# A fused RWKV-5 attention and leaky-ReLU MLP kernel on one core: fewer places for the inputs, more transpose buffers, u loaded by GpSimd, half of pair 0's first products split by chunk, and a new written order

## The chip, the cores and the metric
One core of a Trainium2 chip runs the whole kernel in one launch. The metric is the device time of one execution in microseconds (us), lower is better. The core's engines are TensorE (PE in the profile), VectorE (DVE), ScalarE (ACT), GpSimd (POOL) and SyncE (SP). Each runs its own instruction stream in order, and they wait for one another through semaphores.

## The reference, cut to what matters
There are 4 batches, 8 heads, 768 tokens and a head width of 48. Per batch and head, a 48 x 48 state is carried over the tokens, with r, k, v of the token and w, u of the head:

```
cur   = outer(u * k_t, v_t)
y_t   = r_t @ (state + cur)
state = w[:, None] * state + outer(k_t, v_t)
```

The y of all heads side by side are x (3072 tokens x 384). Then h = x @ w_in (384 x 2048), g = max(0.01 h, h), and the output is g @ w_out (2048 x 384), in float32.

## The kernel before
**Chunks and pairs.** The 3072 tokens are 24 chunks of 128 tokens, six for each batch, named n; two chunks make a pair m of 256 tokens (12 pairs). The recurrence within a chunk is turned into products: r and k are scaled by powers of w (tables qtab and ktab), multiplied to a 128 x 128 score per head, masked, and multiplied by v; the state enters at the chunk's edge.

**The written order.** Every step of the kernel has a letter and numbers, and the string ORDER lists all steps in the order in which they are recorded, for all engines together. Each engine then plays its own steps in that order. The class Sched finds for each step what it reads and overwrites, and adds the semaphore waits. Behind an @ stand the PSUM banks that the step uses; there are eight banks, and a step that opens a bank waits until its last reader is done. The steps, by letter:

- p: the start: tables, constants and first loads (list `first`, L336); q: zero the padding of a qk buffer (DVE, L374); F: filler products on a tile of ones, whose result nobody reads (PE, L381).
- k, r, v: load one chunk by a GpSimd DMA, with a cast to bf16 (L276); i, w: load a quarter of w_in and w_out (L282, L286).
- P: scale r and k of a chunk into qk (DVE, L393; for chunk 0 in two halves, P0.1 for k, L396, and P0.0 for r, L399). T and C: transpose a half on PE (L415) and copy it out (ACT, L426). X: transpose a whole chunk by a DMA from the SP queue instead (L404). Chunks 0 to 7 use T and C, chunks 8 to 23 use X.
- A: scores of a chunk (PE, L475). M: mask them (DVE, L485, L496, L499); for half of chunks 1 and 5, m copies on ACT (L506) and N masks (DVE, L512).
- D, V: the diagonal term of chunks 0 to 5, by a product for PE (DVE, L430) and a scaling of v (DVE, L554). E, f, R, L: the same term for chunks 6 to 23, by two DVE products and a DVE sum (L436, L441, L446) and a GpSimd select that writes it into the score tile (L461).
- K: keys times values (PE, L529, L533, L538). B, W: the new state (DVE, L564, L567, L572). Y: a chunk's output (PE, L603, L607). O: copy it to xT (ACT, L621).
- J and j: x times two 128-column blocks of w_in for a whole pair, six 256-column matmuls (PE, L658), and the leaky ReLU (ACT, L667). G and g: the same for one chunk and four blocks, twelve 128-column matmuls (functions `up_one` and `gate_one`, L627 and L642, not used in this ORDER).
- t, b: sums for a Strassen-like product (DVE, L710, L729). Z and z: its seven products per pair (PE, L760, eight matmuls of 192 columns each) and their additions (ACT L771, L776, DVE L781). o: store (SP L693, the last two chunks in halves, L698).

**Rings.** Buffers are reused in rings whose lengths stand in RINGS: 6 for the scaled r and k (qk), 7 for the transposed ones (tp), 14 places for loaded r and k, and 14 for v. A load into a place waits until the last reader of the chunk that held it is done.

**The start.** Chunk 0's k and r come in float32 through the ACT and SP queues (L264). w comes as a row, is spread over the partitions by a PE product (L306) and becomes the tables by a logarithm and two exponentials (L311, L363, L365), which need exponents made from an iota by GpSimd (L343, L348, L350). u comes as a row on the ACT queue (L338), is cast (L360), spread on PE (L315) and kept by ACT (L320).

Of the kernel before, what the change touches and what calls it, by code (L numbers as in the profile page):

```python
# [12 lines left out]
L = 128  # L13
# [3 lines left out]
HD = H * D  # L17
# [6 lines left out]
RINGS = (6, 7, 6, 6, 6, 3, 3, 8, 14, 14)  # L24
# [23 lines left out]
J2.0@3 r15 M8 J3.6@0 j2.0 v16 J3.4@1 E12 f12 v10 Y9@3 E10 P12 Y8@5 O9 r18 b2.0 X12 J3.0@6 j3.4 E13 O8 Z2.0@3 k17
z0.3 j3.6 f10 f13 J4.7@5 o2 z1.6 R10 k16 j3.0 J4.1@4 z0.5 R13 L10 J3.7@2 j4.1 K12@1 k15 J4.4@0 j3.7 B12 z2.0
J4.0@4 b3.0 j4.7 k19 b2.1 A10@12 j4.0 A11@56 r14 Z2.1@7 j4.4 M11 L13 Z2.2 M10 J4.6@4 k21 J4.2@0 j4.6 b2.3 k23  # L50
J4.5@5 z2.1 j4.2 b2.2 J4.3@6 j4.5 K9@4 z2.2 Z2.3@2 j4.3 B9 R12 A13@01 A12@45 M13 L12 Z3.0@6 Z2.4 z3.0 r21 W9 M12
Z2.5 v20 K10@0 Z3.1@1 B10 v18 z2.5 Y12@4 z3.1 Y10@5 W10 O12 b3.1 Y13@0 v14 Y11@7 P15 O13 K13@4 k18 O10 b4.0 Z3.2
O11 z2.3 J6.0@0 v21 E15 z3.2 z2.4 J6.6@5 f15 v17 b4.1 Z3.3@7 B13 r17 J5.1@2 b3.2 Z2.6 r16 P14 j6.0 b3.3 j5.1
J5.3@4 b4.2 Z3.4 j5.3 P18 J6.2@0 E17 E14 J5.0@2 b4.3 j6.2 J5.5@4 R15 z2.6 o5 f14 Z3.5 L15 X14 j5.5 R14 J6.3@0
j5.0 z3.4 E19 v15 P16 J6.1@3 X15 f19 L14 Z4.0@4 j6.1 Z3.6 o1 W13 X16 J6.4@2 P17 z3.6 j6.6 P19 J5.7@3 j6.4 E18 o7
K14@6 f18 Z4.1@5 j5.7 X18 z3.5 B14 j6.3 J5.4@2 z3.3 z4.0 E16 z4.1 J5.6@3 o4 W14 o0 Z4.2 j5.6 X19 A14@01 z4.2
A15@67 j5.4 M14 J5.2@3 X17 Z4.3@2 j5.2 R19 J6.7@0 M15 L19 Z4.4 k20 b5.0 K18@1 Y14@3 B18 Y15@6 R18 Z5.0@7 O15 f16
O14 b6.2 Z4.5 z5.0 j6.7 z4.4 J7.7@1 R16 Z4.6 f17 L16 z4.5 z4.3 J6.5@6 R17 o8 L18 J7.5@0 E20 o6 j6.5 o3 z4.6
A16@23 k22 j7.7 A18@56 M16 J7.2@4 L17 J7.1@1 j7.2 M18 J7.0@2 r23 j7.1 K15@3 J7.3@4 b6.0 j7.0 r20 j7.5 B15 A17@12
v19 A19@56 j7.3 b5.1 J7.4@0 M17 Z5.1@3 j7.4 Z5.2 W15 K16@4 Z6.0@0 z5.2 B16 Z6.1@1 b5.2 z6.0 z5.1 b5.3 J7.6@2 M19  # L60
Z5.3@4 j7.6 Z5.4 W16 P23 Y16@2 b6.1 Y19@5 O16 X23 Y17@6 P20 Y18@2 O17 z5.4 Z5.5 f20 O19 z5.3 O18 Z5.6 b6.3 Z6.2
# [102 lines left out]
def bass_rwkv5_eagle__then__act_leaky_relu_kernel(  # L164
# [24 lines left out]
    u_row = SB("u_row", [1, HD], FP32)  # L189
# [5 lines left out]
    k0_f = SB("k0_f", [128, HD], FP32)  # L195
    r0_f = SB("r0_f", [128, HD], FP32)
# [7 lines left out]
    u_row16 = SB("u_row16", [1, HD])  # L204
    one_row16 = SB("one_row16", [1, 128])
# [53 lines left out]
    def load_first(which):  # L259
        src = {"k": k, "r": r}[which][0].rearrange("h t d -> t h d")[0:L, :, :]  # L260
        dst = {"k": k0_f, "r": r0_f}[which]
        eng = {"k": "act", "r": "sp"}[which]
        queue = {"k": A, "r": SP}[which]
        add(eng, lambda: queue.dma_start(dst[:, :].rearrange("p (h d) -> p h d", d=D), src),  # L264
            W=[(which, 0)], dma=f"{which}0")
# [25 lines left out]
    def row(h):  # L291
        return dram(h, 0, [[HD, 1], [1, HD]])
# [571 lines left out]
```

## Time and profile before

| what | value |
|---|---|
| median of 3 runs | 165.91 us (165.53 to 166.29) |
| the profiled execution's own time | 166.21 us |
| its span in the profile | 164.1 us (2.1 us lie around it) |
| TensorE busy | 157.8 us, 96% |
| VectorE busy | 130.8 us, 80% |
| ScalarE busy | 88.6 us, 54% |
| GpSimd busy | 89.0 us, 54% |

Busy time is the time in which at least one instruction of the engine is shown running. In the timeline, a row is the start, the duration, the engine, the line, the operation, the tile written and the tile read, and how many instructions were merged; in brackets stands how long the engine had been idle before it, and what ended that. Names ending in q (SPq, POOLq) are an engine's DMA issues. PEld is the load of a matmul's stationary operand. The chain of waits is the chain of work that ended last, followed back from the end.

### The profile page before, as it was taken

The page shows a single profiled execution, that of the slowest core. Times are in us where ns is not written, and L with a number is a line of the kernel's source. Part 1 is how long each engine was busy: PE and PEld are TensorE (multiplying, and loading weights), DVE is VectorE, ACT ScalarE, POOL GpSimd, SP SyncE. Part 2 cuts the span into 40 slices and gives each one's busy share as a digit, 9 for nine tenths or more (in the row PEclk, how much of TensorE's full clock was granted, in tenths as well). Part 3 has the DMA queues.
Part 4 walks back from the last instruction along what each step waited for, and adds up shares of the span by engine and source line. Part 5 has one row for each costly group of instructions (what it writes and reads, how often), then busy time and mean ns, then how long its engine had stood idle before and what let it go on. Part 6 is the DMA issues. An engine that isn't in the chain of part 4 may idle for free.

```text
span 164.1 us, 5320 instructions
## 1 busy us (share of the span) xinstructions
PE 157.8 (96%) x2283; PEld 137.3 (84%) x2283; DVE 130.8 (80%) x261; ACT 88.6 (54%) x195; POOL 89.0 (54%) x101
## 2 busy tenths in 40 slices
PE   4899999999999899999999999999999999999993
PEld 1356778888999688899998988998989998999993
DVE  2579996999997998999997979899769960514771
ACT  3558569954862367623668256453673625738220
POOL 7999999599949969599360469000491000000000
PEclk9999999999999999999999999999999999999999
DMA  6999999999999999959999979935980000034116
GB/s 104 114 147 154 160 174 176 202 191 147 141 142 198 123 139 185 100 30 110 88 151 270 221 123 105 56 67 112 225 46 6 4 0 4 0 121 173 47 32 213
DMA packets 100091, 19.68 MB, mean 120 GB/s; under 512 B 93154, under 2 KB 100068, under 8 KB 100068
## 3 DMA queue, kind: packets, MB, share of 16 engines
q0 software_dynamic: 76512, 10.03, 93.5%
q1 hardware_dynamic: 22226, 8.92, 24.9%
q10 hardware_dynamic: 1330, 0.39, 1.0%
q8 instruction: 18, 0.29, 0.7%
q14 instruction: 5, 0.04, 0.1%
HBM read 20.45 MB, written 4.72 MB: 153 GB/s over the span
## 4 chain that ended last, share of the span: by engine, by line
PE 93%; DVE 2%; DMA 2%; issue 1%; ACT 0%; ACTq 0%; DVEq 0%
PE ps_all L658 39%; PE ps_all L760 33%; PE ps_all L603 6%; PE ps_all L475 4%; PE ps_all L381 4%; PE ps_all L415 3%; PE ps_all L533 2%; DMA u_row<-in_u_dram 2%; PE ps_all L607 1%; DVE out_sb L781 1%; DVE qk L393 1%; PE ps_all L529 0%; ACT u_row L360 0%; PE ps_all L315 0%; DVE sum_t L567 0%
## 5 line engine op out<-in xcount | busy, mean ns | idle before, releaser
L658 PE MATMUL ps_all<-xT,w_in_sb 128*128 128x256 bf16 x576 | 71.8, 273 | 0.0
L667 ACT ACTIVATE gT<-ps_all 128x512 bf16<-128x512 f32 x96 | 54.2, 604 | 31.4 <-PE ps_all L658 25.0
L658 PEld LDWEIGHTS ps_all<-xT,w_in_sb 128*128 128x128 bf16 x576 | 54.1, 98 | 6.8 <-DVE at L499 0.2
L461 POOL TENSOR_SCALAR_AFFINE_SELECT at<-s_tok 128x1024 bf16<-128x1024 f32 x18 | 21.3, 1195 | 33.8 <-DVE s_tok L446 33.7
L760 PE MATMUL ps_all<-tw,gs 128*128 128x192 bf16 x288 | 28.2, 246 | 0.0
L760 PEld LDWEIGHTS ps_all<-tw,gs 128*128 128x128 bf16 x288 | 24.0, 98 | 0.4
L499 DVE CAST_PREDICATED at<-mask,ps_all 128x1024 bf16<-128x1024 uint16 x18 | 21.5, 1216 | 2.1 <-PE ps_all L475 1.1
L781 DVE TENSOR_TENSOR out_sb<-ps_all,snap 128x192 f32<-128x192 f32 x37 | 12.5, 351 | 13.1 <-PE ps_all L760 12.9
L276 POOL DMA_DIRECT2D v_sb<-in_v_dram x24 | 22.1, 943 | 0.0
L729 DVE TENSOR_TENSOR gs<-gT 128x1024 bf16<-128x1024 bf16 x24 | 18.2, 765 | 4.6 <-ACT gT L667 4.6
L276 POOL DMA_DIRECT2D rk_sb<-in_r_dram x23 | 21.3, 939 | 0.3 <-issue 0.3
L276 POOL DMA_DIRECT2D rk_sb<-in_k_dram x23 | 21.1, 939 | 0.0
L771 ACT ACTIVATE snap<-ps_all 128x192 f32<-128x192 f32 x36 | 11.3, 333 | 18.0 <-PE ps_all L760 17.9
L760 PE MATMUL ps_all<-w_out_sb,gT 128*128 128x192 bf16 x192 | 19.3, 246 | 0.0
L621 ACT ACTIVATE xT<-ps_all 128x384 bf16<-128x384 f32 x24 | 11.1, 496 | 10.4 <-PE ps_all L603 8.6
L760 PEld LDWEIGHTS ps_all<-w_out_sb,gT 128*128 128x128 bf16 x192 | 15.9, 98 | 0.7
L393 DVE TENSOR_TENSOR qk<-rk_sb,tab 128x768 bf16<-128x768 bf16 x23 | 15.3, 685 | 0.0
L426 ACT ACTIVATE tp<-ps_all 128x512 bf16<-128x512 f32 x16 | 9.0, 604 | 5.0 <-PE ps_all L415 5.0
L603 PE MATMUL ps_all<-at,v_sb 128*32 128x128 bf16 x384 | 10.5, 220 | 0.1
L603 PEld LDWEIGHTS ps_all<-at,v_sb 128*32 128x32 bf16 x384 | 8.2, 96 | 2.4 <-issue 1.3
L760 PE MATMUL ps_all<-w_out_sb,gs 128*128 128x192 bf16 x96 | 9.9, 246 | 0.0
L446 DVE TENSOR_REDUCE s_tok<-ku 128x8 f32<-128x384 bf16 x18 | 9.7, 544 | 0.1
(69 smaller groups left out, 184.3 us busy)
## 6 DMA issues: line engine op xcount, KB each, us to landing
out_dram<-out_sb SPq DMA_DIRECT2D x22, 192.0 KB, 2.2
v_sb<-in_v_dram POOLq DMA_DIRECT2D x24, 96.0 KB, 5.0
rk_sb<-in_r_dram POOLq DMA_DIRECT2D x23, 96.0 KB, 5.2
rk_sb<-in_k_dram POOLq DMA_DIRECT2D x23, 96.0 KB, 5.3
w_in_sb<-in_moe_w_in_dram POOLq DMA_DIRECT2D x4, 384.0 KB, 5.9
w_out_sb<-in_moe_w_out_dram POOLq DMA_DIRECT2D x4, 384.0 KB, 10.3
tp<-qk SPq DMA_TRANSPOSE x16, 4.3
k_f<-in_k_dram ACTq DMA_DIRECT2D x1, 192.0 KB, 2.9
```

The costliest lines, as they stand in the source:

```text
L276: add("pool", lambda: G.dma_start(dst, src), W=[key], dma=f"{which}{n}")
L393: add("dve", lambda: V.tensor_tensor(qk[iq][:, :, 0:D], both, by, ALU.mult), R=[("r", n % NRK), ("k", n % NRK), "qtab", "ktab", ("qk0", iq ...
L461: add("pool", lambda: G.affine_select(out=at[ia][:, :, :, :].rearrange("p two m i -> p (two m) i"), in_=s_tok[i2][:, :].unsqueeze(2).to_br ...
L499: add("dve", lambda: V.copy_predicated(dst, mask[:, :].bitcast(mybir.dt.uint16).unsqueeze(1).to_broadcast([128, H, 128]), raw), R=keys + [ ...
L603: last = PE.matmul(ps_y[32 * q:32 * q + 32, 128 * s:128 * s + 128], a, m, start=first_mm and (s == 0 or whole), stop=last_mm and whole)
L621: add("act", lambda: A.activation(xT[m % NX][:, :, 128 * half:128 * half + 128], ps[i][:, 0:HD].rearrange("p (s t) -> p s t", t=128), AF.C ...
L658: last = PE.matmul(ps[i][:, 256 * f:256 * f + 256], w_in_sb[:, s, 128 * fb:128 * fb + 128], xT[ix][:, s, :], start=s == 0, stop=s == NSL - 1)
L667: add("act", lambda: A.activation(gT[ig][:, 2 * j:2 * j + 2, :].rearrange("p f t -> p (f t)"), ps[i][:, :], AF.Prelu, alpha=0.01), R=[key] ...
L729: add(eng, lambda: on.tensor_tensor(x[i][:, :, :], a, b, op), R=keys, W=[("gs", m % 2, i)])
L760: done = PE.matmul(ps[i][:, 0:NH], lhs[:, s, :], rhs[:, s, :], start=bool(opens) and s == 0, stop=s == HF - 1, skip_group_check=not (opens ...
L771: add("act", lambda: A.activation(snap[i2][j][:, :], ps[i][:, 0:NH], AF.Copy), R=[key], W=[("snap", i2, j)])
L781: add("dve", lambda: V.tensor_tensor(out_sb[io][:, cols], ps[i][:, 0:NH], snap[i2][j][:, :], ALU.add), R=[key, ("snap", i2, j), *after], W ...
```

## The change
- RINGS go from (6, 7, 6, 6, 6, 3, 3, 8, 14, 14) to (8, 10, 6, 6, 6, 3, 3, 8, 10, 12): qk 8 for 6, tp 10 for 7, places of r and k 10 for 14, of v 12 for 14.
- u is no longer a row that ACT casts, PE spreads and ACT copies. One GpSimd DMA reads it 128 times into u_tab, with the cast.
- Chunk 0's float32 k and r land in output tiles 5 and 4 instead of tiles of their own.
- J0.0 to J0.3 and their j become G0.0, G0.1, G1.0, G1.1 and their g: blocks 0 to 7 for chunk 0 and chunk 1 separately.
- ORDER is new throughout: the order of the steps on every engine, and the banks. The fillers are 17 with 4864 columns for 28 with 9728.

```diff
-RINGS = (6, 7, 6, 6, 6, 3, 3, 8, 14, 14)
+RINGS = (8, 10, 6, 6, 6, 3, 3, 8, 10, 12)
+FIRST = {0}
 ORDER = """
-p3 p0 p9 p12 q0 p2 p18 p1 r3 p11 p13 p14 p10 p4 p8 p5 p21@0 k3 p6 p20 k1 p7 p25@1 F1.256.0@2 p22 r1 F1.128.4@3
-F1.128.5@4 F1.512.8@2 p24 F1.256.12@0 k2 F1.512.15@7 P0.1 F1.256.4@0 F1.512.16@2 p17 r2 p27 p15 p23 p19 q5
-F1.512.4@0 q4 q3 F1.512.6@7 P0.0 i1 p28 F1.256.9@0 p16 T0.1@2 v0 T0.0@0 F1.512.12@3 C0.1 p32 p31 F1.512.7@4 q1
-F1.512.0@3 k5 C0.0 P1 p29 A0@23 D0 p30 r5 F1.512.5@0 q2 M0.0 F1.256.16@7 F1.512.19@6 T1.0@0 v1 P2 F1.128.2@4
...
+p3 p0 p19 p10 r1 p2 p8 p16 p4 r2 p11 p5 p21@0 p6 k1 p7 F1.512.12@1 k2 F1.128.19@2 p22 F1.512.18@1 F1.128.3@7 i1
+F1.128.21@6 F1.128.17@5 F1.256.4@7 F1.512.17@0 p9 v0 F1.512.11@1 p13 q0 p24 p18 q1 F1.128.7@0 F1.512.1@7 q5 p14
+p31 p17 p23 k3 p15 F1.128.6@6 P0.1 F1.128.0@7 F1.256.5@5 p27 F1.512.6@4 p28 P0.0 r3 F1.256.9@3 q2 T0.0@2 P1
+T0.1@1 C0.0 F1.128.8@0 P2 v1 T1.0@7 T1.1@0 C0.1 k5 C1.0 D0 A0@12 p32 T2.0@6 C1.1 q3 M0.0 T2.1@7 r5 p29 p30 q4
+M0.1 C2.1 v2 K0@5 C2.0 A1@01 D1 V0 m1.1 i0 A2@67 B0 Y0@4 v3 P3 O0 M1.0 K1@5 k4 N1.1 T3.1@1 G0.1@0 V1 C3.1 r4
+T3.0@2 P5 Y1@1 C3.0 i3 D2 B1 A3@23 O1 k7 M2 g0.1 K2@4 T5.0@5 v4 G1.1@1 C5.0 V2 r7 D3 Y2@0 M3.1 i2 T5.1@7 M3.0
+G0.0@6 C5.1 r6 B2 K3@5 O2 G1.0@7 g1.1 V3 p1 q7 Y3@4 P4 k6 B3 T4.0@3 O3 T4.1@2 v6 D5 A5@01 C4.1 q6 J1.0@5 M5.0
...
+j6.7 A15@45 j6.5 A14@67 J6.4@2 M14 j5.6 K14@0 J6.3@3 j6.4 P22 z4.0 J6.1@6 j6.3 M15 X22 J6.2@7 j6.1 Z4.1@2
+P17 j6.2 X18 R18 Z4.2 R19 L18 K15@3 B14 Z4.3@4 z4.2 X20 z4.1 W14 r23 Z4.4 B15 Z4.5 z4.3 L19 X17 R16 Y15@0 z4.4
+v20 Y14@7 b6.0 O15 X16 A18@34 O14 E17 A19@56 v16 M18 Z4.6 K18@0 v17 o3 J7.3@7 z4.6 b6.1 o4 o7 J7.2@1 L16 b5.0 o2
...
+z8.6 Z9.5 o17 z9.4 Z11.0@0 b11.2 Z10.1@5 z9.5 z11.0 b11.1 Z11.1@7 b10.3 Z10.2 Z11.2@3 z10.2 z11.1 z10.1 Z10.3@2
+z11.2 b11.3 Z10.4 Z10.5 z10.4 Z10.6 z10.5 z10.3 Z9.6 z10.6 Z11.3 z9.6 o19 Z11.4 z11.3 o18 z11.7 o16 Z11.5 z11.4
+o23.1 o21 Z11.6@2 o20 z11.5 o23.0 o22.1 z11.6 o22.0
 """
...
+    def early(which, n):
+        return out_sb[4 + 2 * n + (which == "k")][:, :]
...
-    def load_first(which):
+    def load_early(which, n, eng):
...
+    def first_u():
+        add("pool", lambda: G.dma_start(u_tab[:, :], dram(u, 0, [[0, 128], [1, HD]])), W=["u_tab"], dma="u")
...
-    def spread_u():
-        i, key = opened("u")
-        add("pe", lambda: PE.matmul(ps[i][:, 0:HD], one_row16[:, :], u_row16[:, :], start=True, stop=True),
-            R=["one_row16", "u_row16"], W=[key, "bc16"])
-
-    def keep_u():
-        i, key = banks["u"]
-        add("act", lambda: A.activation(u_tab[:, :], ps[i][:, 0:HD], AF.Copy), R=[key], W=["u_tab"])
```

In the new ORDER, GpSimd's iota (p9) stands behind five loads (r1, r2, k1, k2, i1); in the old one it stood ahead of all loads.

More of the change, by code (lines that the diff above doesn't have):

```diff
@@ L52 @@
[L52 to L61, printed above, removed]
@@ L306, in spread_w @@
         add("pe", lambda: PE.matmul(ps[i][:, 0:HD], one_row[:, :], w_row[:, :], start=True, stop=True),
-            R=["one_row", "w_row"], W=[key, "bc"])
+            R=["one_row", "w_row"], W=[key])
     def log_w():
@@ L359, in bass_rwkv5_eagle__then__act_leaky_relu_kernel @@
         lambda: add("dve", lambda: V.memset(wu[:, :, :], 0.0), W=["wu"]),
[L360 removed]
+        None,
         spread_w,
```

103 lines of the change are left out of this document (50 added, 53 removed).

## The prediction

> **What bounds the kernel now.** I read the page's busy shares and chain of waits, then busy time by stretches, then the timeline where the stretches show something.
>
> ```profile
> PE 157.8 (96%) x2283; PEld 137.3 (84%) x2283; DVE 130.8 (80%) x261; ACT 88.6 (54%) x195; POOL 89.0 (54%) x101
> ...
> PE 93%; DVE 2%; DMA 2%; issue 1%; ACT 0%; ACTq 0%; DVEq 0%
> ```
>
> PE is busy for 96% of the span and makes 93% of the chain that ended last: a change pays where it takes work off PE or lets it wait less. The stretches (us; busy us of PE, PEld, DVE, ACT, POOL, with instructions) show where:
>
> ```profile
> 8.51:24.40 15.89, 15.80 (x271) 11.00 (x269) 14.64 (x34) 10.35 (x21) 15.89 (x19) 1.00 2.08 159
> 24.40:108.80 84.40, 83.76 (x1315) 74.76 (x1313) 78.45 (x145) 48.73 (x106) 59.03 (x64) 1.00 1.57 141
> 108.80:161.59 52.79, 52.76 (x688) 49.17 (x688) 33.58 (x68) 25.95 (x62) 6.50 (x6) 1.00 0.32 72
> ```
>
> The first stretch begins with the first real product. After it PE is idle for 0.64 us in 84.40 and 0.03 in 52.79. In the middle stretch DVE works 78.45 us and is idle for only 5.95: **a second limit stands close behind PE**. After 108.80 DVE has 19 us to spare. The first stretch looks full of PE work too, but its rows with L381 are filler, which nobody reads:
>
> ```profile
> by line: PE ps_all L381 42.3%; PE ps_all L415 27.6%; PE ps_all L475 13.8%; PE ps_all L533 4.5%; PE ps_all L603 4.2%; PE ps_all L529 3.8%; PE ps_all L607 3.2%; issue 0.7%
> ...
> 9.36 1.28 PE ps_all L381 x3
> ...
> 11.10 0.65 PE ps_all L381 x3
> 11.74 0.22 PE ps_all L415 x4
> ...
> 15.37 0.36 PE ps_all L603 x16
> ```
>
> This is the chain from 8.51 to 17.1, after which no filler comes; its first row gives L381 42.3% of 8.59 us, so 3.63 us. The others are pieces of it: start, us, line, instructions. The fillers cover waits for the pipeline of a chunk (transpose, copy, scores, mask, output). Dropping them gains nothing unless real work takes their place.
>
> **The change, step by step.** *Half of the first products per chunk.* J0.0 to J0.3 need xT of chunks 0 and 1; G0.0 and G0.1 need chunk 0 alone. A J is six matmuls of 256 columns, a G twelve of 128:
>
> ```profile
> 23.74 0.66 PE ps_all L658 x6
> ...
> 44.50 0.66 PE ps_all L760 x8
> ...
> 107.29 1.51 PE ps_all L603 x100
> ```
>
> A J takes 0.66, four 128-column matmuls 0.22 (row 11.74), so a G 3 x 0.22 = 0.66: no PE time is won or lost, and ACT still does four leaky ReLUs of 128x512. What it brings is a date.
>
> *The start.* Both tables need exponents from the iota, which now stands behind five loads on GpSimd.
>
> ```profile
> 0.90 0.23 POOL L343 IOTA ramp<- 128x128 f32 x1 [0.39 <-POOLq L849]
> 1.41 1.04 POOL L276 DMA_DIRECT2D rk_sb<-in_r_dram  x1 [0.27 <-issue]
> 2.44 1.76 POOL L276 DMA_DIRECT2D rk_sb<-in_k_dram  x2
> 5.12 0.61 ACT L365 ACTIVATE tab<-lnw,kexp 128x384 bf16<-128x384 f32 x1
> ...
> 6.44 0.51 DVE L352 TENSOR_SCALAR ident<-ramp 128x128 bf16<-128x128 f32 x1
> ```
> ```profile
> 2.34 1.64 PE L306 MATMUL ps_all<-w_row,one_row 1*128 1x384 f32 x2 [2.34 <-DMA w_row<-in_w_dram]
> 4.70 0.49 PE L315 MATMUL ps_all<-u_row,one_row 1*128 1x384 bf16 x1 [0.71 <-ACT u_row L360]
> ```
>
> Loads follow each other by 1.03 or 0.88 (half of 1.76). Five from 0.95 on end at 0.95 + 1.03 + 4 x 0.88 = 5.5, and the iota at 5.75, for 1.13. ktab (0.61) then ends at 6.5 for 5.73. DVE has small memsets, the mask and ident (0.51 in its row) ahead of chunk 0's two scalings, which then run at about 7.3 and 7.8 for 0.5 each, and the transposes T0 start at 8.35, for 8.51. The new fillers ahead of them, 4736 columns, fit: at the 0.83 ns per column of row 9.36 (1536 columns in 1.28) they take 3.9 us from the end of the w product (2.34 + 1.64 = 3.98). Bounds of T0's start: 7.9 (the fillers' end) to 9.4 (ident's 0.51 for each of the small ones). I take 8.35, to which the row of the old scalings is nearest.
>
> *The first chunks, walked along.* Start to start DVE needs, from these rows, 0.46 for V (14.72 to 15.18) and P, 0.47 for B, 0.34 for D and as much for N, 0.61 for a half M (17.77 to 18.38) and at most 1.21 for a whole one; ACT needs 0.51 per copy (2.06 for four) and 0.37 per wl; a load of v lands 5.0 us after its issue in the median, 10.9 at most:
>
> ```profile
> 14.72 0.55 DVE L554 TENSOR_TENSOR vs<-v_sb,ps_all 128x384 bf16<-128x384 bf16 x1
> 15.18 0.55 DVE L564 TENSOR_TENSOR st<-ps_all,wl 128x384 bf16<-128x384 f32 x1
> 15.65 0.55 DVE L393 TENSOR_TENSOR qk<-rk_sb,tab 128x768 bf16<-128x768 bf16 x1
> 16.11 0.42 DVE L430 TENSOR_TENSOR prod<-tp 128x512 bf16<-128x512 bf16 x1
> 16.45 0.42 DVE L512 TENSOR_TENSOR at<-at,mask 128x512 bf16<-128x512 bf16 x1
> ...
> 17.77 0.68 DVE L485 TENSOR_TENSOR at<-ps_all,mask 128x512 bf16<-128x512 f32 x1
> 18.38 0.55 DVE L564 TENSOR_TENSOR st<-ps_all,wl 128x384 bf16<-128x384 f32 x1
> 18.84 1.21 DVE L496 TENSOR_TENSOR at<-ps_all,mask 128x1024 bf16<-128x1024 f32 x1
> ```
> ```profile
> 10.08 0.74 ACT L327 ACTIVATE wl<-lncol 48x192 bf16<-48x192 f32 x2
> ...
> 12.93 2.06 ACT L426 ACTIVATE tp<-ps_all 128x512 bf16<-128x512 f32 x4 [0.33 <-PE ps_all L415]
> ```
> ```profile
> DMA to landing us min/median/max: 3.1/5.0/10.9
> ```
>
> T0 (0.44 for both halves, by row 11.74) ends at 8.8, its copies at 9.8, A0 at 10.15. DVE masks A0 until 11.6, then D1 and V0 until 12.4. ACT copies chunk 1, makes wl, copies chunk 2 until 12.5; A2 stands ahead of Y0 on PE, so Y0 runs from 12.85 to 13.45 (15.37 to 16.00 before), its copy ends at 14.0, and G0.1 starts at 14.1. From there DVE sets the pace: V1 ends at 14.75 and Y1 at 15.8; P5 (whose r lands near 15.2: issued near 10.1), D2 and B1 end at 16.5, M2 and V2 at 18.1, Y2 at 18.9; D3, M3, B2 and V3 at 20.5, Y3 at 21.45. G1.1, G0.0 and G1.0 lie in the gaps; A5 ends at 21.8. The old kernel has done the same products (chunks 0 to 3, A5, four units of w_in) when its fourth J ends, at 23.74 + 0.66 = 24.40. **PE is 2.6 us ahead.** Bounds: 3.63 if all filler turns into progress; nothing if the start slips by one and each of some eight hand-overs costs 0.2 more than I gave.
>
> *The middle.* Up to the last Y of chunks 16 to 19 (row 107.29 ends at 108.80) the old order has 42 Z, the new one 39, at 0.66 each (row 44.50); otherwise PE has the same. So PE needs 83.76 - 1.98 = 81.8 us from 21.8 on: 103.6 if it never waits. DVE has, at 21.8, not yet done what it had at 24.40: N5.1, E6, P6, part of D5 and P7, some 1.3 us; up to those Y the new order has two b less and an E and a P more, 0.5 less (between 0 and 1; the b are the longer ones). So it must work 78.45 + 1.3 - 0.5 = 79.3 us, and only 81.8 - 79.3 = **2.5 us of idle** are left to it, for 5.95 before. DVE's idle time was waiting for PE; both in-order streams rarely wait for nothing, so I take the middle, 4.2 us: 21.8 + 79.3 + 4.2 = 105.3. PE's one visible stop of before is an instance of the coupling:
>
> ```profile
> 53.36 1.93 DVE L393 TENSOR_TENSOR qk<-rk_sb,tab 128x768 bf16<-128x768 bf16 x1
> 53.74 1.12 POOL L461 TENSOR_SCALAR_AFFINE_SELECT at<-s_tok 128x1024 bf16<-128x1024 f32 x1
> ...
> 55.61 0.40 PE L475 MATMUL ps_all<-tp 48*128 48x128 bf16 x8 [0.62 <-DVE out_sb L781]
> ```
>
> DVE's P took 1.93 us instead of 0.55 beside GpSimd's select, so a bank came free late and PE stood for 0.62. The Trainium skill (SBUF — State Buffer, section "Who interferes with whom") says that a DVE instruction with two SBUF inputs and a GpSimd one that reads SBUF take one lock, held for the whole instruction; these rows agree. By that rule alone the two orders could be told apart by what stands right behind each sum R on DVE: a two-SBUF-input step 10 times in 18 before, 8 times now, which would save DVE about 1 us; the sum does without it.
>
> *The rest.* After those Y, 52.79 + 1.98 = 54.8 us follow to the last product, then 164.10 - 161.59 = 2.5 to the end. On the SP queue five whole stores now stand within the last four Z, ahead of the last half, for three before: two more of 192 KB, between 0 and 1 us later; I take 0.2, since they are issued earlier.
>
> *At nothing.* u by GpSimd: a load's 0.9 us on GpSimd, issued at about 20.5 and wanted by E7 near 28; it takes a product of 0.49 off PE (row 4.70), ahead of fillers, and would cost only if it landed over 7 us later. Chunk 0 in output tiles: the outputs that overwrite them come 40 us later. Two more zero memsets on DVE, 0.3, lie in its idle time. More qk and tp buffers free SP of waits that PE didn't feel. Fewer places: each load after the start goes out at least 6 us of PE work ahead of its use, for a median landing of 5.0; the longest, 10.9, would be felt by a few.
>
> **Sum.** Y17 at 105.3 + 54.8 + 2.5 + 0.2 = span 162.8, that is 1.3 less than 164.1. The profiled execution took 166.21, the median is 165.91: I predict **164.6** for the median.
>
> **The rivals.**
> (a) PE never waits: span 103.6 + 57.5 = 161.1, time 162.9. For it: the old order kept PE waiting for 0.64 only. Against: DVE would have to be 97% busy for 82 us. Chance 0.15.
> (b) DVE waits as much as before, 5.95: 107.05 + 57.5 = 164.55, time 166.35: the gain of the start given back. The point is 5.5 us of idle. Chance 0.17.
> (c) Slower: the DMA transpose of chunk 18. Between X18 and A18 PE has four Z, K15, Y15 and Y14, 4 x 0.66 + 0.2 + 2 x 0.45 (four Y take 1.51 in row 107.29) = 3.7 us; the shortest such distance in the old order is 5.7.
>
> ```profile
> L404 SPq DMA_TRANSPOSE tp<-qk x16: 1236/1304/1995, 47.2 to 115.0; - x16
> ...
> DMA to landing us min/median/max: 3.2/4.3/6.1
> ```
>
> Issue takes 1.3 us, landing 4.3 in the median and 6.1 at most, and four others go out around it. From a landing of 3.7 + 1.3 = 5.0 the gain is gone; at 6.1 PE stands for 2.4 us: span 165.2, time 167.0, and more if chunk 18's masks then hold up the neighbours'. Chance 0.20.
> (d) PE stays slow longer. Row 9.36 has 0.83 ns per column, row 11.10 0.51 (1280 columns), though PEclk shows 1.00 throughout; PE had been busy without a gap from 4.7 to 10.64. The new start has gaps of some 0.4 to 0.9 us from 9.4 on. If it runs at half speed until 15, 4.0 us of products become 8.0, and 2.3 are lost: time 166.9; up to 168.6 if until 18. The Trainium skill (TensorE: Matmul & The Clock Gate, Part 1) says that the clock is halved until a window of 3.4 us was busy, and again after an idle one; by that rule the new fillers, without the old gap of 0.71 ahead of row 4.70, have PE at full rate by 9.4, which is nearly what the walk takes. Chance 0.08.
> (e) The change doesn't do what it says: the G wait for w_in. The quarter wanted at 14 is the fifth load, issued by 5.5: no weight.
>
> **How the numbers follow.** The forecast has 0.40 and by itself reaches from 163.4 to 165.4. A measurement tells about 0.5%, 0.83 us, from no change. Faster by more: (a) and three quarters of the forecast, and little of the rest, 0.47. Within: the rest of the forecast and most of (b), 0.23. Slower: (c), (d), some of (b), 0.30. The range reaches from (a), less 0.7 for a start that is earlier by its bound and stores that cost nothing, 162.2, to the upper end of (d), 168.6.
>
> **What would show it.** Right: L381 filler after the first transpose near zero, G0.1 near 14, Y3's end near 21.5, DVE idle of 3 to 5 us between there and Y17. Wrong: a PE wait for T0 after 9.4; A18 late behind a DMA; PE idle over 3 us after 25.

## The result: 174.1 us, slower by 4.9%

The changed kernel takes **174.10 us** (median of 4 runs, 173.35 to 175.30), the kernel before beside it 165.72 (165.51 to 166.29): ratio 1.0494, 95% interval 1.0449 to 1.0539. Predicted were 164.6 us, between 162.2 and 168.6. The profiled execution took 173.35 with a span of 171.6. Ratios are formed from the runs within 1.5% of the fastest of the same kernel, but medians and ranges are of all runs, since the changed order spreads by 3% by itself (171.2 to 176.6 us in e13 below).

Busy shares and the chain of waits of the changed kernel, from its page:

```profile
PE 156.0 (91%) x2295; PEld 137.8 (80%) x2295; DVE 127.8 (74%) x262; ACT 88.8 (52%) x193; POOL 90.2 (53%) x102
...
PE 46%; DVE 23%; DMA 16%; POOL 7%; issue 5%; ACT 1%; DVEq 0%; POOLq 0%
PE ps_all L754 19%; PE ps_all L652 19%; DMA tp<-qk 9%; DMA rk_sb<-in_k_dram 6%; DVE gs L723 4%; DVE qk L387 4%; PE ps_all L597 3%; POOL rk_sb L278 3%; PE ps_all L469 2%; DVE at L493 2%; POOL at L455 2%; DVE tw L704 2%; POOL v_sb L278 2%; DVE ku L430 1%; DVE sum_t L561 1%
```

PE no longer carries the chain: 46% for 93% before. DMAs have 16% of it: the DMA transposes (tp<-qk) have 9%, loads of k 6%. Line numbers are six lower than before (L652 is J, L754 Z, L597 Y, L469 A, L387 the scaling P, L398 the DMA transpose), and in most of the experiments eight lower.

Stretches as in the prediction (us; busy us of PE, PEld, DVE, ACT, POOL, then granted clock): from the end of A5 to the last Y of chunks 16 to 19, and from there to the last product.

```profile
22.60:111.01 88.41, 82.99 (x1284) 74.19 (x1284) 77.96 (x146) 48.27 (x106) 64.34 (x69) 0.98 1.78 151
111.01:167.62 56.61, 55.02 (x712) 51.10 (x710) 32.86 (x69) 27.39 (x63) 4.43 (x4) 1.00 0.16 41
```

Laid beside the prediction's own sum, stage by stage:

| stage | predicted | profile after | difference |
|---|---|---|---|
| to the end of A5 | 21.8 | 22.60 | +0.8 |
| A5 to the last Y of chunks 16 to 19 | 83.5 | 88.41 | +4.9 |
| to the last product | 54.8 | 56.61 | +1.8 |
| to the end of the span | 2.7 | 171.6 - 167.62 = 4.0 | +1.3 |
| span | 162.8 | 171.6 | +8.8 |

In the middle PE is idle for 88.41 - 82.99 = 5.42 us (0.64 before), in the third stage for 1.59 (0.03). DVE was to be the second limit there; it worked 77.96 us (79.3 forecast) and was idle for 10.45. The largest piece, in order of time on PE (start, us, line, operation, count, idle time before):

```profile
54.06 0.33 PE L527 MATMUL ps_all<-v_sb,qk 128*128 128x96 bf16 x4
58.11 0.62 PE L469 MATMUL ps_all<-tp 48*128 48x128 bf16 x16 [3.71 <-DMA tp<-qk]
58.66 1.45 PE L652 MATMUL ps_all<-xT,w_in_sb 128*128 128x256 bf16 x6
59.91 1.48 PE L754 MATMUL ps_all<-w_out_sb,gT 128*128 128x192 bf16 x8
61.19 1.28 PE L754 MATMUL ps_all<-tw,gT 128*128 128x192 bf16 x8
62.40 0.28 PE L469 MATMUL ps_all<-tp 48*128 48x128 bf16 x4
```
```profile
58.66:62.40 3.74, 3.74 (x25) 3.02 (x24) 2.82 (x3) 0.93 (x2) 3.74 (x5) 0.54 1.70 146
62.40:66.00 3.60, 3.60 (x94) 3.15 (x94) 3.09 (x4) 1.21 (x3) 1.95 (x3) 1.00 2.02 148
```

The scores of chunk 9 wait 3.71 us for their DMA transpose. Behind the stop one J and two Z take 62.40 - 58.66 = 3.74 us where 3 x 0.66 would do, and the second view says why: the granted clock was 0.54 there and 1.00 afterwards. The stop costs 3.7 + 1.8 us. The six DMA transposes of chunks 8 to 13, before and after (issue ns min/median/max, first and last start; us to landing):

```profile
L404 SPq DMA_TRANSPOSE tp<-qk x6: 1236/1295/1937, 47.2 to 59.2; - x6
...
DMA to landing us min/median/max: 4.1/4.9/6.1
```
```profile
L398 SPq DMA_TRANSPOSE tp<-qk x6: 1391/2551/4057, 44.3 to 57.7; - x6
...
DMA to landing us min/median/max: 6.8/8.6/9.5
```

They go out 3 us earlier, are issued half as fast and take almost twice as long. When the first goes out, 10 loads of r, k and v are issued but not landed; 5 were before (counted from each load's issue and landing in the trace).

The third stage and the end belong together: the stores. SP issues eight whole rows in a block, while the load of k23 is under way.

```profile
99.76 7.17 SPq L687 DMA_DIRECT2D out_dram<-out_sb  x8
```
```profile
L278 POOL DMA_DIRECT2D rk_sb<-in_k_dram x1: 919/919/919, 101.9 to 101.9; - x1
...
  DVE ku L430: 3.1, 1
...
DMA to landing us min/median/max: 11.0/11.0/11.0
```
```profile
119.13 0.83 PE L754 MATMUL ps_all<-w_out_sb,gT 128*128 128x192 bf16 x8 [1.15 <-DVE sum_t L561]
...
121.06 0.61 PE L652 MATMUL ps_all<-xT,w_in_sb 128*128 128x256 bf16 x4 [0.44 <-DVE sum_t L561]
```

k23 lands 11.0 us after its issue, DVE stands 3.1 us for it, the state sums come late, and PE stops for 1.15 + 0.44 = the 1.59 us of the third stage.

### The profile page after: what moved, and what is told of

Read it like the earlier page. It is cut to its first block, busy times and chain, and to the rows that moved or that the text cites. A ratio compares the mean times of both kernels' runs of the same rounds, so it can differ in the third digit from the quotient of the medians.

```text
span 171.6 us, 5349 instructions
## 1 busy us (share of the span) xinstructions
PE 156.0 (91%) x2295; PEld 137.8 (80%) x2295; DVE 127.8 (74%) x262; ACT 88.8 (52%) x193; POOL 90.2 (53%) x102
## 4 chain that ended last, share of the span: by engine, by line
PE 46%; DVE 23%; DMA 16%; POOL 7%; issue 5%; ACT 1%; DVEq 0%; POOLq 0%
PE ps_all L754 19%; PE ps_all L652 19%; DMA tp<-qk 9%; DMA rk_sb<-in_k_dram 6%; DVE gs L723 4%; DVE qk L387 4%; PE ps_all L597 3%; POOL rk_sb L278 3%; PE ps_all L469 2%; DVE at L493 2%; POOL at L455 2%; DVE tw L704 2%; POOL v_sb L278 2%; DVE ku L430 1%; DVE sum_t L561 1%
## 5 line engine op out<-in xcount | busy, mean ns | idle before, releaser
L661 ACT ACTIVATE gT<-ps_all 128x512 bf16<-128x512 f32 x92 | 51.9, 603 | 32.8 <-PE ps_all L652 31.0
L652 PE MATMUL ps_all<-xT,w_in_sb 128*128 128x256 bf16 x552 | 66.6, 274 | 0.4 <-DVE sum_t L561 0.4
L652 PEld LDWEIGHTS ps_all<-xT,w_in_sb 128*128 128x128 bf16 x552 | 52.5, 98 | 7.8 <-DVE sum_t L561 0.7
L455 POOL TENSOR_SCALAR_AFFINE_SELECT at<-s_tok 128x1024 bf16<-128x1024 f32 x18 | 22.1, 1244 | 26.2 <-DVE s_tok L440 26.1
L754 PE MATMUL ps_all<-tw,gs 128*128 128x192 bf16 x288 | 28.2, 246 | 0.0
L754 PEld LDWEIGHTS ps_all<-tw,gs 128*128 128x128 bf16 x288 | 24.1, 98 | 0.2
L754 PE MATMUL ps_all<-w_out_sb,gT 128*128 128x192 bf16 x192 | 20.3, 251 | 1.2 <-DVE sum_t L561 1.2
L775 DVE TENSOR_TENSOR out_sb<-ps_all,snap 128x192 f32<-128x192 f32 x37 | 12.2, 348 | 9.5 <-PE ps_all L754 7.6
L615 ACT ACTIVATE xT<-ps_all 128x384 bf16<-128x384 f32 x24 | 10.8, 494 | 15.4 <-PE ps_all L597 13.5
L754 PEld LDWEIGHTS ps_all<-w_out_sb,gT 128*128 128x128 bf16 x192 | 16.5, 100 | 2.0 <-DVE sum_t L561 1.4
L469 PE MATMUL ps_all<-tp 48*128 48x128 bf16 x192 | 8.3, 218 | 6.3 <-DMA tp<-qk 5.0
L387 DVE TENSOR_TENSOR qk<-rk_sb,tab 128x768 bf16<-128x768 bf16 x23 | 12.4, 543 | 1.1 <-DMA rk_sb<-in_r_dram 1.1
L469 PEld LDWEIGHTS ps_all<-tp 48*128 48x128 bf16 x192 | 5.5, 94 | 8.7 <-issue 4.1
L597 PE MATMUL ps_all<-at,v_sb 128*32 128x128 bf16 x384 | 10.6, 220 | 0.5 <-DMA v_sb<-in_v_dram 0.4
L754 PE MATMUL ps_all<-tw,gT 128*128 128x192 bf16 x96 | 10.2, 253 | 0.0
```

The source lines that it names most:

```text
L387: add("dve", lambda: V.tensor_tensor(qk[iq][:, :, 0:D], both, by, ALU.mult), R=[("r", n % NRK), ("k", n % NRK), "qtab", "ktab", ("qk0", iq ...
L455: add("pool", lambda: G.affine_select(out=at[ia][:, :, :, :].rearrange("p two m i -> p (two m) i"), in_=s_tok[i2][:, :].unsqueeze(2).to_br ...
L469: last = PE.matmul(ps[i][:, 128 * p:128 * p + 128], tp[it][at_rows, NP + p, :], tp[it][at_rows, p, :], start=True, stop=True)
L597: last = PE.matmul(ps_y[32 * q:32 * q + 32, 128 * s:128 * s + 128], a, m, start=first_mm and (s == 0 or whole), stop=last_mm and whole)
L652: last = PE.matmul(ps[i][:, 256 * f:256 * f + 256], w_in_sb[:, s, 128 * fb:128 * fb + 128], xT[ix][:, s, :], start=s == 0, stop=s == NSL - 1)
L661: add("act", lambda: A.activation(gT[ig][:, 2 * j:2 * j + 2, :].rearrange("p f t -> p (f t)"), ps[i][:, :], AF.Prelu, alpha=0.01), R=[key] ...
```

## The experiments

Theory: the new order puts DMA transposes into a backlog of loads, and loads behind a block of stores. Rivals: the smaller number of places; DVE as the bound; the new start. "Outstanding" are loads of r, k and v that are issued and have not landed when the first transpose goes out. A ratio is to the kernel before, run beside the experiment. Each profile shows one execution.

**e1, e14: more places.**
```diff
-RINGS = (8, 10, 6, 6, 6, 3, 3, 8, 10, 12)
+RINGS = (8, 10, 6, 6, 6, 3, 3, 8, 13, 14)
```


> The changed kernel, its order untouched, with 13 places for r and k instead of 10 and 14 for v instead of 12. Theory (order of the transfers: DMA transposes stand on the SP queue and in time where the loads are still backed up, and stores ahead of late loads): GpSimd no longer waits for places (4.3 us for r22 and 2.6 us for v22 in the changed kernel), but loads only go out earlier; PE's stop before A9 near 54 us stays at 3 to 4.5 us, the stops near 118 to 121 stay within 1 us of 1.6, and the time stays at 172.5 to 175.5. Rival (fewer places): the stops after 80 us go and the stop before A9 shrinks under 1.5 us, time 167 to 170.

Measured: 171.13 us (169.95 to 171.68), ratio 1.0302 (1.0237 to 1.0367). A9 did not wait at all (the longest stop of PE between 40 and 66 us was 0.30, before A11), against the theory; the late stops stayed (1.04 and 0.44), against the rival. But in that execution the fourth chunk's output was copied at 23.7 us instead of 21.9, and the first transpose went out at 46.2 with 7 loads outstanding. That left it open, and e13, e14 and e15 were put side by side on one chip.

> The changed kernel itself, once more, beside e14 and e15 on one chip. Theory (a lead of PE at the start brings the first DMA transposes forward into a backlog of loads that the DMA engines set): 172.5 to 175.5; the number of loads outstanding when X8 is issued, and the landings of X8 to X13, follow the lead of this execution as in the others (10 or 11 outstanding: over 6.8 us; 7: 4.4 to 7.7).

> e1 once more. Theory (places bind only after 65 us, and e1's missing stop before A9 came from a shorter lead in that execution): 171 to 174, at most 2 us under e13. Rival (places are worth the 3 us that e1 showed): 169.5 to 171.7, 2.5 to 4 us under e13 in all runs.

Measured: e13 174.27 us (171.16 to 176.60), e14 173.24 (171.72 to 174.98). The same six transposes, e13 and then e14:

```profile
L398 SPq DMA_TRANSPOSE tp<-qk x6: 1342/2501/4642, 46.2 to 61.0; - x6
...
DMA to landing us min/median/max: 6.7/9.0/10.1
```
```profile
L396 SPq DMA_TRANSPOSE tp<-qk x6: 1346/2518/3724, 46.1 to 59.1; - x6
...
DMA to landing us min/median/max: 6.6/8.4/9.1
```

10 and 9 loads outstanding, stops before A9 of 4.23 and 3.31 us: with 13 and 14 places the stop is there all the same. The places cannot have set it: up to r12, at 45.7 to 45.8 us, GpSimd issues every load at the same time within 0.12 us in e1, e13 and e14. Nor did the lead of PE, which both theories name, tell these three apart: the first transpose went out at 46.1 or 46.2 us in each. What differed is when the loads landed: w0, issued at 23.6 us in each, landed at 31.4 in e1, at 34.4 in e13 and at 33.6 in e14. The times leave open what places are worth behind A9. e14 is 1.0 us under e13, and all ten runs of e1 and e14 have a median of 171.9 us, those of the changed kernel and e13 174.3.

**e2: fewer places in the old order** (11 and 12 for 14 and 14 in the kernel before).

> The kernel before, its order untouched, with 11 places for r and k and 12 for v instead of 14 each (with 10, r22 would stand ahead of the last use of r12 in this order). Theory (order of the transfers): within 1 us of the kernel before, 165 to 167. Rival (fewer places): a good part of the 8 us of loss shows, 168 us or more, with waits of GpSimd on places and PE stops behind late loads.

Measured: 166.65 us, before 166.13; ratio 1.0028 (0.9996 to 1.006). As the theory said: in the old order the places alone cost nothing that can be told.

**e15, e9: three loads later.**
```diff
 order of GpSimd's loads
-r13 v13 k10 k8 r8 r9 k11 k9 r10 r11 r16 v8 v9 v12 k12 r12 v10 k16 k19 r19 v19 v11
+r13 k10 k8 r8 r9 k11 k9 r10 r11 v8 v9 k12 r12 v10 k16 k19 r19 v19 v11 v12 r16 v13
```


> The changed kernel with three loads that are wanted late (v13, r16, v12) moved behind v11 on GpSimd, out of the backlog ahead of the first DMA transposes; nothing else. So far the transposes of chunks 8 to 13 took 3.5 to 6.1 us to land where 5 or 6 loads were outstanding at the issue of the first, 4.4 to 7.7 with 7, 6.8 to 8.0 with 8, 6.8 to 9.5 with 10 and 7.3 to 11.0 with 11. Theory (transposes among outstanding loads land late): 7 or 8 outstanding here, landings of 4.4 to 8 us, PE's stop before A9 under 2 us, and 1.5 to 4 us less than the changed kernel: 170 to 172.5. Rival (it is the order of X13, X8, X9 on the SP queue, or a place, that holds A9): 173 to 175 with a stop over 3 us.

Measured: 174.09 us (171.41 to 183.65). Its profiled execution, the one of 183.65, had a granted clock of 0.85 nearly throughout, so its times can't be compared, but its transposes of chunks 8, 9, 10 and 13 landed in 3.1 to 3.5 us with 4 loads outstanding. Hence once more:

> e9 once more, whose profiled execution had a granted clock of 0.85 and can't be read for times. Theory (backlog of loads ahead of the first transposes): 4 to 8 loads outstanding at X8, landings of X8 to X13 under 6 us but for X11, X12, no stop before A9 over 1 us, 1.5 to 4 us under e13. Rival: within 1 us of e13.

Measured: 171.57 us (170.79 to 172.80), 2.7 under e13 by the medians; one run of e13 lies in the same range, and the ratios, 1.0281 (1.0227 to 1.0336) and 1.032 (1.022 to 1.042) in e13, don't tell the two apart. The transposes in e15:

```profile
L396 SPq DMA_TRANSPOSE tp<-qk x6: 1234/1340/2616, 45.7 to 55.8; - x6
...
DMA to landing us min/median/max: 3.8/5.7/7.7
```

The first issue is as in e13 within 0.5 us, on the same queue, in the same order; 7 loads are outstanding instead of 10. The median landing falls from 9.0 to 5.7, the issue time from 2.5 to 1.3 us, and the longest stop at a score product from 4.23 to 0.66. It was not a quicker execution: r13, issued at 28.3 us, landed at 41.6 as in e14, but chunk 9's transpose landed at 53.5 us for 59.3 there. **The backlog of loads makes the transposes late.** In all four executions with the three loads moved (e9, e15, e10, e16) A9 never waited; of the five with these loads, the order of the transposes and PE's work as in the changed kernel, four waited for 3.31 to 5.20 us (the changed kernel, e8, e13, e14) and one did not (e1). Across all executions of the changed order and its variants, landings (min to max of the six) rise with the loads outstanding:

| kernel | loads outstanding | to landing, us | longest PE stop, 40 to 66 us |
|---|---|---|---|
| before | 5 | 4.1 to 6.1 | 0.62 |
| e9 (clock 0.85) | 4 | 3.1 to 5.9 | under 0.1 |
| e10 | 6 | 3.4 to 7.3 | 0.49 |
| e1, e15, e16 | 7 | 3.7 to 7.7 | 0.56 |
| e4 | 8 | 6.8 to 8.0 | 3.0, filled |
| e14 | 9 | 6.6 to 9.1 | 3.31 |
| after, e13 | 10 | 6.7 to 10.1 | 4.23 |
| e7, e8 | 11 | 7.3 to 11.0 | 5.20 |

The gain in time is less sure than the mechanism: all ten runs of e9 and e15 have a median of 171.9 us, no less than those with more places.

**e4: filler in the stop.** 14 products of 512 columns, read by nobody, ahead of A9.
```diff
-j3.7 B8 r19 K9@6 z1.5 j3.6 A9@23
+j3.7 B8 r19 K9@6 z1.5 j3.6 F14.512.0@2 A9@23
```


> The changed kernel with 14 products of 512 columns that nobody reads put on PE just ahead of the scores of chunk 9 (3.0 us at full rate, inside the stop of 3.7 us). Theory (the wait is for the transpose's landing, and PE runs slow after the stop): the scores of chunk 9 start at the same time, but the J and Z after them take 0.66 per six and eight matmuls at once instead of 1.38 and 1.18, so the time falls by 1 to 2 us, to 172 to 173. Rival (the products after the stop are slow for another reason, a bank or operand): no change, 173.5 to 174.5; and if PE's own work were what A9 waited for, the time would rise by 3.

Measured: 172.92 us (171.41 to 173.55), 1.2 under the changed kernel's median. PE there:

```profile
55.71 2.97 PE L373 MATMUL ps_all<-ones 128*128 128x512 bf16 x13
58.61 0.62 PE L467 MATMUL ps_all<-tp 48*128 48x128 bf16 x16
59.16 0.83 PE L650 MATMUL ps_all<-xT,w_in_sb 128*128 128x256 bf16 x6
59.83 0.82 PE L752 MATMUL ps_all<-w_out_sb,gT 128*128 128x192 bf16 x8
60.49 0.82 PE L752 MATMUL ps_all<-tw,gT 128*128 128x192 bf16 x8
61.24 0.40 PE L467 MATMUL ps_all<-tp 48*128 48x128 bf16 x8
```

A9 starts at 58.61 (58.11 without filler), and the J and two Z behind it go by every 0.66 us at a granted clock of 1.00: behind filler instead of a stop, the stop's second cost, the slow clock, falls away. That useless work shortens the kernel is not shown. In this execution chunk 9's transpose had landed at 56.8 us, so that A9 would have waited for 1.1 us and the filler held it back for 1.8; and the times lie within the spread of the changed kernel (171.16 to 176.60 with e13).

**e7: X13 moved.**
```diff
 SP's queue
-X8 X13 X9 X10 X11 X12
+X8 X9 X10 X11 X12 X13
 DVE: P13 likewise behind P12
```


> The changed kernel with the scaling and the DMA transpose of chunk 13 moved behind those of chunk 12; nothing else. Theory (A9 waits for a transpose that stands behind two others among the loads): X9 goes out in X13's old place, 2.7 us sooner, and lands near 54; PE's stop before A9 falls from 3.7 to under 1.2 us and the slow products behind it go; time 169 to 171.5. Rival (fewer places, or the backlog of loads alone): X9 lands as late as before, near 58; 173 to 175.

Measured: 174.88 us (170.53 to 175.26). X9 went out 0.6 us sooner than in the changed kernel, landed at 55.2 instead of 58.0, and A9 no longer waited. But the time stayed, for another stop of 2.95 us took its place, before A10 (59.0 to 62.0 us). DVE, then GpSimd:

```profile
56.40 3.21 DVE L385 TENSOR_TENSOR qk<-rk_sb,tab 128x768 bf16<-128x768 bf16 x2
59.54 1.24 DVE L564 TENSOR_TENSOR st<-sum_t,wl 128x384 bf16<-128x384 bf16 x1
60.70 2.34 DVE L491 CAST_PREDICATED at<-mask,ps_all 128x1024 bf16<-128x1024 uint16 x2
```
```profile
58.06 2.50 POOL L453 TENSOR_SCALAR_AFFINE_SELECT at<-s_tok 128x1024 bf16<-128x1024 f32 x2
```

The scalings of chunks 12 and 13 take 3.21 us (twice 0.55 alone), 2.35 of it the second, which with the state product of 1.24 (0.35 alone) runs beside two selects of GpSimd from 58.06 to 60.56; the mask on which a bank hung came late. It is the stretching that the prediction showed for one P of 1.93 us. The theory was right on A9 and wrong on the time: mending one transpose only moved the stop. Whether the 11 loads outstanding or the new place of the scaling brought it there is not shown.

**e8: stores earlier.**
```diff
 SP's queue
-X8 X13 X9 X10 X11 X12 X21 X15 X14 X19 o1 o0 X22 X18 X20 X17 X16 o3 o4 o7 o2 o5 o9 o6 o8 X23 ... o17 o19 o18 o16 o21 ...
+X8 X13 X9 X10 X11 X12 o3 o2 o0 o1 o4 o5 X21 X15 X14 o6 X19 o7 X22 X18 X20 X17 X16 o9 o8 X23 ... o16 o17 o18 o19 o21 ...
```


> The changed kernel with the whole-row stores on the SP queue moved to where their rows are ready: o0 to o3 and o4, o5 into the gap of the SP queue between 60 and 80 us, o6, o7 among the transposes, o16 and o18 ahead of o19; nothing else. Theory (stores that go out in a block delay what is behind them): k23 lands within 7 us instead of 11, the stops near 118 and 121 (1.15 and 0.44 us) go, and the end comes 2.6 us after the last product instead of 4.0; 2 to 3 us less, 171 to 172.5. Rival (those loads are late because GpSimd waits for places): stops and time stay but for the end, 172.5 to 174.5.

Measured: 171.53 us (169.28 to 172.68), ratio 1.0185 (1.0095 to 1.0274). The load of k23:

```profile
L276 POOL DMA_DIRECT2D rk_sb<-in_k_dram x1: 919/919/919, 104.8 to 104.8; - x1
...
DMA to landing us min/median/max: 5.3/5.3/5.3
```

5.3 us for 11.0. In all eight executions that keep the block of stores k23 takes 10.3 to 11.3 us, in the three without it (e8, e10, e16) 5.0 to 5.9. There is no stop after 109 us; the span ends 170.81 - 167.90 = 2.9 us after the last product for 4.0. As the theory said, 2.6 us less by the medians, although its profiled execution had the longest stop before A9 of all (5.20 us).

**e10, e16: loads and stores; and places besides.**

> The changed kernel with both: the three loads of e9 later and the stores of e8 earlier. Theory (two separate losses, one of backlog ahead of the transposes, one of stores ahead of late loads and at the end): the gains add up, 1.5 to 4 from the one and 2.6 to 3.6 from the other: 167 to 170, with no stop over 0.6 us after O15. Rival (the same loss, which moves from place to place): no better than the better of the two, 170 to 172.5.

> e10 (three loads later, stores earlier) with 13 places for r and k and 14 for v. Theory (with ten places GpSimd waits 4.3 us for the place of r22 and all loads behind it, and P14 and P15 with their transposes are late: e10 still stops 1.17 us for X14 and 0.60 for v11): those stops fall under 0.5 us each and the time is 1 to 2 us under e10: 167.4 to 168.4. Rival (the place is not what those loads wait for): 169 to 170, the stops stay.

Measured: e10 169.39 us (168.55 to 171.73), ratio 1.0128 (1.0038 to 1.0218); e16 169.68 (168.40 to 170.41), ratio 1.0157 (1.01 to 1.0214). The two gains add up (4.7 us under the changed kernel), and places add nothing on top: the rival of e16 holds. The edits are those of e9 and e8, in e16 with the places of e1. What is left of the loss in e16 are waits of one to two us with different causes (us in total, times, longest):

```profile
PE ps_all L521 <- DMA v_sb<-in_v_dram: 1.8, 1, 1.8
PE ps_all L467 <- DMA tp<-qk: 1.0, 2, 0.8
PE ps_all L752 <- DVE gs L721: 0.9, 1, 0.9
PE ps_all L467 <- DVE s_tok L438: 0.9, 1, 0.9
```

Two of them end with DVE, the prediction's second limit.

**e3, e5, e6, e11: the new start with the old rest.**
```diff
 e3
-RINGS = (8, 10, 6, 6, 6, 3, 3, 8, 10, 12)
+RINGS = (6, 7, 6, 6, 6, 3, 3, 8, 14, 14)
 new order as far as g1.0
-the rest of the new order
+j1.0 j1.2 j1.3, then all other steps as the kernel before has them, without J0.0 to J0.3
```

> The new start and first half of pair 0's products (u by GpSimd, chunk 0 in output tiles, G instead of J, everything up to the mask of chunk 5), then all remaining steps in the order of the kernel before, with the places and buffers of the kernel before (14, 14, 6, 7). Theory (order of the transfers from 40 us on): the start's lead of about 1.8 us survives, no PE stop over 1.5 us after 25 us; time 163.5 to 166. Rival (DVE is the bound and takes the lead back): 165.5 to 167 with PE stops spread over the middle and DVE idle under 4 us. Rival (the new start itself costs): 168 or more, with the stops after 25 us.

Measured: 169.73 us, ratio 1.024 (1.0167 to 1.0313). The theory's range is missed at the joint, where the two orders meet: E6 stands early in the old order, while its load k6 stands late in the new one.

```profile
29.20 0.36 DVE L428 TENSOR_TENSOR ku<-rk_sb,u_tab 128x384 bf16<-128x384 bf16 x1 [4.61 <-DMA rk_sb<-in_k_dram]
```

DVE stood 4.61 us, PE 3.14, and PE's granted clock was 0.50 from 30.42 to 36.00. After that there is no stop over 0.30 us.

```diff
 e5: the new order as far as f6 (for g1.0), then as e3
 e6: besides, GpSimd's first loads
-r1 r2 k1 k2 i1 (iota) v0 k3
+r1 r2 k1 k2 v0 i1 (iota) k3
```


> As e3, but the new order is kept until the second product of chunk 6's sum (f6, about 37 us), so that E6 and P7 come only after their loads; from there on all remaining steps in the order of the kernel before, places and buffers of before. Theory (the loss sits in the transfers of the new order from 43 us on, and e3's stop was its joint, where E6 asked for k6 eight loads too early): no PE stop over 1 us after 25 us, chunks 16 to 19 done 0 to 2 us ahead of the kernel before; time 164 to 166. Rival (the new start costs later whatever follows, since DVE or the loads take the lead back): 166.5 or more, with stops in the middle.

> e5 with one load moved: v of chunk 0 goes out ahead of the first quarter of w_in instead of behind it. Theory (the start is set by landings: the first K waits for v0, 0.3 to 1.3 us in the runs so far, and the gap makes the products after it slow): v0 lands near 9 us, the gap before the first K shrinks to what DVE needs, output of chunk 0 is copied before 13.9 us every time; 0.3 to 1.2 us less than e5. Rival (that gap is hidden by what DVE does next): same time as e5 within 0.3 us.

Measured: e5 166.13 us, ratio 0.9968 (0.9932 to 1.0005); e6 166.07, ratio 0.9962 (0.9932 to 0.9993). With the rest in the old order the 8 us are gone, though e5 comes out 0.1 above the theory's range. In e6 v0 lands at 9.5 us for 12.2 and the first K no longer waits for it, but the time is that of e5: the rival. The edit has a price of its own: the iota now stands behind one load more, and T0 starts at 9.08 us for 8.21.

```diff
 e11: as e6, and
-GpSimd: k13 v7 w2 w1 w3 r13 v13 k10 k8 k9
+GpSimd: k8 v7 w2 w1 w3 r13 k9, with k10, k13, v13 as in the kernel before
-PE: J0.5 A7 A6 Y5
+PE: A7 A6 Y5 J0.5
-DVE: E8 t0 t2 t1 E9 t3
+DVE: t0 t2 t1 E9 t3 E8
```


> e6 (new order up to f6, old order for the rest, v0 first) with the joint mended: k8, k9, k10, k13, v13 loaded in the old sequence, J0.5 behind Y5, E8 behind the sums of w_out. Theory (PE work lost at the joint, 0.58 + 0.69 + 0.20 us of stops, comes back in full because nothing else is late): 0.8 to 1.5 us less than e6, 164.6 to 165.4. Rival (DVE or the transposes take it back between 45 and 60 us): 165.7 to 166.3.

Measured: 165.67 us (165.23 to 166.64), kernel before beside it 166.17; **ratio 0.9959 (0.992 to 0.9997)**. It lies between the two ranges. It is 0.4 us under e6 on another chip, but by the ratio to the kernel before beside it (0.9962 in e6) the mended joint gains nothing that can be told, though the profiled span fell by 0.9. It clearly beats the changed kernel, and the one before by 0.4%, with an interval that just excludes no change. Most of the start's lead is gone by the end; where it goes stays open.

**e12: the iota first.**
```diff
 e11, GpSimd
-r1 r2 k1 k2 v0 i1 (iota) k3 r3 v1 k5 r5 v2
+(iota) r1 k1 v0 k2 r2 v1 i1 k3 r3 v2 r5 k5
```

> e11 with the start in another order: the iota first on GpSimd, then r1, k1, v0, k2, r2, v1, and w_in only then; the small steps of DVE in the order in which they are wanted, and the fillers ahead of the first transpose cut from 4736 to 3328 columns. Theory (with the iota behind the loads the exponent table, and with it the first transpose, is late by 1.5 us): T0 starts near 6.6 instead of 8.2 to 9.1 us, and what the loads of chunks 1 to 5 allow of it remains: 0.3 to 1.5 us less than e11. Rival (the loads' landings set the first 24 us, whatever the start): the same time as e11 within 0.3 us.

Measured: 166.39 us, ratio 0.9992 (0.995 to 1.0033). T0 starts at 6.68 us (9.09 in e11), chunk 0's output is copied at 13.7 (14.6), but chunk 1's at 17.9 (17.2). The time is 0.7 us above e11, outside both ranges, and the rival's mechanism holds: in this execution DVE waits for loads of r, for 1.41 us until 9.00 and for 1.14 until 14.15, and in e11 for no load from 5 to 24 us. The loads of the first chunks set the pace, not the table.

## Why the prediction was wrong, point by point

- **J to G costs no PE time:** right. 24 matmuls of 256 columns have become 48 of 128, and the profile has G0.1 at 14.43 (14.1 forecast).
- **The start and the walk:** right in the profile of the changed kernel, and no more than that. T0 at 8.21 (8.35), chunk 3's output copied at 21.86 for 23.86 before, A5's end at 22.60 (21.8). But the lead of 2.0 us at chunk 3 is the best of the executions with this start; e13 has 0.1, e1 0.2, e15 0.7. The walk left out a load: the first K needs v0.

```profile
12.33 0.24 PE L523 MATMUL ps_all<-wu,prod 128*128 128x2 bf16 x4 [1.60 <-DMA v_sb<-in_v_dram]
```
```profile
14.40:18.20 3.80, 3.76 (x58) 3.28 (x59) 3.73 (x7) 1.41 (x3) 3.80 (x6) 0.55 1.83 165
```

  In e13 v0 lands at 12.2 us (10.9 in the changed kernel's first profile), and after the gap the granted clock is 0.55 for 3.8 us: rival (d), which had 0.08, in part. It is no rarity: of the 16 profiled executions with the new start, eight have a mean granted clock of 0.72 or less from 12 to 18.2 us (e1, e3, e5, e9, e10, e13, e14, e16) and eight have 1.00, the changed kernel's own among them.
- **The middle, 83.5 us:** the work was nearly right (DVE 77.96 us for 79.3, PE 82.99 for 81.8, where the slow clock behind A9 alone costs 1.8), the waiting wrong. The forecast left PE 83.5 - 81.8 = 1.7 us to wait, all of it by the coupling of DVE and PE; it waited 5.42, of which 5.0 for DMA transposes and 0.4 for a load of v.
- **The step that failed:** the sum has no term for waiting for transfers. "At nothing" says why: "each load after the start goes out at least 6 us of PE work ahead of its use, for a median landing of 5.0". It took the landing as a constant of the old profile, for loads and transposes alike. In the changed kernel transposes land after 6.5 us in the median instead of 4.3, loads of k after 8.1 (5.3) and stores after 3.4 (2.2), because the same transfers meet in other company: 3.7 + 1.8 us were lost at A9, 1.59 behind k23 and 1.3 at the end. Fewer places themselves, which the sentence was about, cost nothing that can be told in the old order (e2) or beside e10's moves (e16); in the changed order some 2 us are not excluded (e1 and e14), none of it before A9.
- **A row that was not read:** the page's row DMA, the mean busy share of the core's 16 DMA engines in tenths, in 40 slices of the span, before and after:

```profile
DMA  6999999999999999959999979935980000034116
```
```profile
DMA  7999999999999999999995999910321001200127
```

  In the kernel before it shows 9 in every slice from 4 to 70 us. Whether the DMA engines were full, the row does not say; but they had transfers under way nearly all the time in the stretch in which the new order moves loads and transposes about. The prediction's stretches hold the same share behind the clock (1.57 from 24.40 to 108.80; times of packets are added up, so it can pass 1), and it was not read.
- **Rival (c)** was the right kind of mechanism at the wrong place. It priced chunk 18, where the distance on PE was shortest (in the profile A18 does not wait); the backlog stood ahead of chunk 9. Its bound for the landing, 6.1, was the old maximum. The slow clock behind a stop belonged to its price as well.
- **The rest:** two more stores near the end were put at 0.2; stores cost 1.59 us at k23 and 1.3 more at the end (e8 gives 2.6 of that back).
- **Rivals (a), (b), (e)** did not decide: PE waited more, not less; DVE was idle for 10.45 us, but the longest pieces are 2.95 and 1.25 at masks behind A9's stop, 1.44 for the scores of chunk 4 and 1.09 for a load of r; w_in came in time.

What sets the transfer rate of one execution (v0, issued at 6.0 us, lands between 10.8 and 12.4 in the changed order) stays open; nothing was tried on it. With it stays open why one execution of the same program has 7 loads outstanding and the next one 9.

## What to carry to other kernels

The time from issue to landing is no property of a transfer but of the queue it meets: for every reordered DMA count what is issued and not landed at its new place, transposes beside loads above all. A lead won at the start is worth nothing where the loads set the date (e12). And a stop of PE must be priced with the slow clock behind it.

## What the runs showed of the hardware that I had not expected

- **A stop is paid twice.** After 3.71 us the granted clock was 0.54 for 3.7 us, after e3's 3.14 it was 0.50 for 5.6. After e13's 1.60 us the products ran at 1.00 for 2.1 us and only then at 0.55 for 3.8; after e15's 1.52 us the clock stayed at 1.00. In e1 two stops of 0.59 and 0.55 us, at 11 to 13 us, were followed by 0.50 from 13.2 to 16.5. The Trainium skill (TensorE: Matmul & The Clock Gate, Part 1) has the clock halved after an idle window of about 3.4 us that runs freely; the half rate agrees, and so, roughly, does its length of 3.7 and 3.8 us, though not e3's 5.6; but here stops of well under a window were enough, in some executions.
- **Transposes and loads slow each other.** In the changed kernel loads land 0.7 us apart before the first transpose's issue ends at 45.69 (r8, r9, k11, k9 from 42.88 to 45.08), and v9, v12 and k12 2.3 apart (48.64, 50.96, 53.34) beside three transposes. The Trainium skill (DMA: Bandwidth & Descriptors, section "Queues, rings and completion order") says that each DMA engine goes round between the queues that have work, a packet at a time; these rows agree.
